# Strassen block products for the first product of tiles 2 to 8, with the weights' sums streamed from DRAM and the attention one pair ahead

## The chip, the core and the metric

The kernel runs on one core of a Trainium2 chip. A core has five engines that run their own instruction queues in order and wait for each other by semaphores: TensorE (PE in the profile; PEld are its weight loads), VectorE (DVE), ScalarE (ACT), GpSimd (POOL) and SyncE (SP, which here only issues DMAs). SBUF is the on-chip memory, PSUM the memory into which PE accumulates. The metric is the device time of one execution in microseconds (us), as the median of several runs.

## The reference

```python
def _attn_ref(q, k, v):                      # each (8, 8, 576, 64): batch, head, row, column
    q_s = q - np.max(q, axis=-1, keepdims=True)
    q_s = np.exp(q_s)
    q_s = q_s / (np.sum(q_s, axis=-1, keepdims=True) + 1e-09)
    k_s = k - np.max(k, axis=2, keepdims=True)          # over the rows
    k_s = np.exp(k_s)
    k_s = k_s / (np.sum(k_s, axis=2, keepdims=True) + 1e-09)
    kv = np.einsum('bhsd,bhse->bhde', k_s, v)
    return np.einsum('bhsd,bhde->bhse', q_s, kv)

def _moe_ref(x, w_in, w_out):                # x (4608, 512), w_in (512, 2048), w_out (2048, 512)
    h = np.maximum(x @ w_in, 0.0)
    return h * h @ w_out
```

The output of the attention, with heads side by side, is x. The weights come as 64-bit floats.

## The kernel before

The 4608 rows of x are worked off in nine tiles of 512 rows: tile t = 0 to 7 holds the first 512 rows of batch t, tile 8 the last 64 rows of all eight batches, which pass through DRAM (`x_tail`). Every number of the two big products is held as a sum of two 32-bit parts that PE takes in one pass, a high part and the rest (`wi_h`, `wi_l`, `xh`, `xl`, `gh`, `gl`), and each product is made of three matmuls: high times high, high times low, low times high.

A tile is a loop over 16 blocks f of 128 columns of w_in. `first` makes h for a block: 4 slices of 128 rows of w_in by 3 matmuls with 512 columns, 12 in all, into one of two PSUM buffers (pool `ps_h`). ACT and DVE make r = relu(h), h squared, and its parts gh and gl. `second` multiplies them with w_out into four accumulators `acc` that live through the tile; the three matmuls for one f and one accumulator are called a unit here. It runs two f behind (LA = 2), so that 8 units are left at the end of a tile, where `store` empties the accumulators and `split_x` splits the next tile's x.

Between these stands the attention of the next batch, b = t + 1, in four pieces p of two heads; in a tile, piece p belongs to the blocks f = 4p to 4p + 3. From batch 2 on, its steps are these.

- `blocks_max`, `blocks_exp`, `blocks_norm`, `blocks_turn`, `blocks_split`: q's softmax on DVE and ACT, with the halves of a maximum and of a sum exchanged over small DMAs (`sw_m`, `sw_s`), and the split of its transpose in `qh` and `ql` (on POOL where p is even, on DVE where p is odd).
- `k_max` on DVE, then `k_shift_pool` on POOL: an all-reduce over the partitions (`kmx<-km`), and the subtraction of its result from k (`k<-k,kmx`) and from its last rows (`kt`). `k_exp` on ACT turns these into `ek` and `kt`.
- `kv_product` (PE, then ks, kvh, kvl on DVE and ACT) and `x_product` (PE, six matmuls of 288 columns, then copies into x), for two pieces together where p is odd.

Up to the end of tile 0 a planner orders all instructions by costs and due times, with tile 0 in it. From tile 1 on (the planner is then closed) every engine's queue is in the order in which the code is written. All instructions pass through one helper, so that nearly all rows of a profile show the line L100; the tile names tell them apart.

## Time and profile before

| | |
|---|---|
| median of 3 runs | 883.64 us (883.05 to 884.48) |
| span of the profiled execution | 881.9 us |
| PE busy in the span | 865.1 us, 98% |
| DVE, ACT, POOL busy | 485.8, 359.7, 186.8 us |
| moved by DMA | 57.89 MB, 66 GB/s on average |

The span runs from the first to the last instruction of the profiled execution; the runs' times lie around it by some us. In a row of the timeline stand the start, the duration, the engine, the line, the operation, out<-in by names, the shapes, and in brackets the idle time ahead with what ended it ("issue" if nothing that the profile shows). In a row of a group stand the count after the x, then busy us and mean ns of one, then the idle time ahead and what ended most of it. A row of waits has the total, the number and the longest. A matmul's duration holds its latency; what counts on PE is the distance of two starts.

### The profile page before, as it was taken

The numbers are of one execution on the slowest core, as the hardware profiler recorded it, in microseconds if no ns is written. First come the engines' busy times: TensorE is split into PE (matmuls) and PEld (weight loads), VectorE is DVE, ScalarE is ACT, GpSimd is POOL, SyncE is SP. The second block draws the span as 40 slices with busy tenths as digits, with TensorE's granted clock in tenths as the row PEclk, the third lists the DMA queues.
The fourth block names the chain that finished last, engine by engine and source line by source line (L and its number), as shares of the span: only waits on it lengthen the run. The fifth ranks groups of instructions, "written<-read, shape, count | busy, mean of one in ns | idle before, by whom it ended". The sixth has DMA issues, their size and how long they took to land.

```text
span 881.9 us, 12457 instructions
## 1 busy us (share of the span) xinstructions
PE 865.1 (98%) x4456; PEld 714.6 (81%) x4456; DVE 485.8 (55%) x897; ACT 359.7 (41%) x668; POOL 186.8 (21%) x237
## 2 busy tenths in 40 slices
PE   7899999999999999999999999999999999999997
PEld 6678888888888888788888888888888888888886
DVE  6888976554655465545654565556564532233222
ACT  5878854333434342335333343334233422232221
POOL 5789982111111101110111112110111000000000
PEclk9999999999999999999999999999999999999999
DMA  9992122211311122112311222113111110010002
GB/s 262 376 349 70 37 50 73 53 29 37 85 39 39 39 63 80 39 38 57 86 39 39 46 72 48 30 38 93 39 38 39 54 50 1 0 48 1 1 1 48
DMA packets 140878, 57.89 MB, mean 66 GB/s; under 512 B 115600, under 2 KB 134032, under 8 KB 140688
## 3 DMA queue, kind: packets, MB, share of 16 engines
q1 hardware_dynamic: 139104, 55.79, 23.6%
q10 hardware_dynamic: 1712, 1.31, 0.5%
q8 instruction: 35, 0.57, 0.3%
q14 instruction: 27, 0.22, 0.1%
HBM read 46.14 MB, written 10.49 MB: 64 GB/s over the span
## 4 chain that ended last, share of the span: by engine, by line
PE 91%; DMA 3%; DVE 3%; issue 1%; ACT 1%; SPq 1%; POOL 0%; DVEq 0%; POOLq 0%; ACTq 0%
PE acc L100 43%; PE h L100 42%; PE x L100 3%; PE kv L100 2%; DMA q<-in_q_dram 1%; DMA raw<-in_moe_w_in_dram 1%; DMA sw_m<-bmx 1%; SPq L100 1%; DVE km L100 1%; DMA kt<-in_k_dram 0%; DVE w L100 0%; POOL w L100 0%; DVE gl L100 0%; DVE up L100 0%; DVE qt L100 0%
## 5 line engine op out<-in xcount | busy, mean ns | idle before, releaser
L100 PE MATMUL h<-xh,w 128*128 128x512 f32 x1152 | 379.3, 392 | 3.2 <-DVE gl L100 3.1
L100 PE MATMUL acc<-w,gh 128*128 128x512 f32 x1152 | 355.7, 390 | 0.0
L100 PEld LDWEIGHTS h<-xh,w 128*128 128x128 f32 x1152 | 216.2, 188 | 50.3 <-DVE gl L100 4.4
L100 PEld LDWEIGHTS acc<-w,gh 128*128 128x128 f32 x1152 | 214.7, 188 | 43.4
L100 PE MATMUL h<-xl,w 128*128 128x512 f32 x576 | 224.3, 389 | 0.0
L100 PE MATMUL acc<-w,gl 128*128 128x512 f32 x576 | 224.2, 389 | 0.0
L100 DVE SCALAR_TENSOR_TENSOR h<-h,r 128x512 f32<-128x512 f32 x144 | 99.4, 691 | 101.8 <-ACT r L100 101.0
L100 DVE TENSOR_TENSOR gl<-h,gh 128x512 fp32r<-128x512 f32 x144 | 99.2, 689 | 92.2 <-ACT gh L100 83.7
L100 ACT ACTIVATE r<-h 128x512 f32<-128x512 f32 x144 | 85.1, 591 | 152.2 <-PE h L100 151.8
L100 ACT ACTIVATE gh<-r 128x512 fp32r<-128x512 f32 x144 | 90.7, 630 | 122.2 <-PE acc L100 113.7
L100 PEld LDWEIGHTS acc<-w,gl 128*128 128x128 f32 x576 | 108.1, 188 | 22.8
L100 PEld LDWEIGHTS h<-xl,w 128*128 128x128 f32 x576 | 108.2, 188 | 21.3
L100 POOL TENSOR_TENSOR k<-k,kmx 128x512 f32<-128x512 f32 x24 | 30.8, 1282 | 171.9 <-issue 143.1
L100 POOL PARTITION_ALL_REDUCE kmx<-km x24 | 17.4, 724 | 207.4 <-DVE km L100 166.2
L100 ACT ACTIVATE q<-q 128x576 f32<-128x576 f32 (+1 forms) x32 | 21.5, 672 | 96.7 <-DVE q L100 87.9
L100 POOL TENSOR_TENSOR w<-w,raw 128x512 int32<-128x512 int32 x32 | 42.0, 1320 | 7.9 <-DVE w L100 2.8
L100 POOL TENSOR_TENSOR w<-w,w 128x512 fp32r<-128x512 f32 x32 | 41.1, 1299 | 5.8 <-ACT w L100 5.7
L100 DVE SCALAR_TENSOR_TENSOR bsm<-bsm,sw_s 128x18 f32<-128x18 f32 x24 | 5.6, 232 | 61.4 <-DMA sw_s<-bsm 61.4
L100 ACT ACTIVATE raw<-raw 128x1024 f32<-128x1024 f32 (+1 forms) x32 | 36.3, 1148 | 2.2 <-DMA raw<-in_moe_w_in_dram 2.0
L100 DVE TENSOR_TENSOR bmx<-bmx,sw_m 128x18 f32<-128x18 f32 x24 | 4.2, 176 | 53.0 <-DMA sw_m<-bmx 53.0
L100 ACT ACTIVATE kvh<-kv,ks 64x64 fp32r<-64x64 f32 x64 | 19.8, 309 | 29.4 <-DVE ks L100 28.9
L100 ACT CAST qh<-qT 128x576 fp32r<-128x576 f32 (+1 forms) x32 | 20.9, 653 | 26.2 <-DVE qT L100 24.6
(104 smaller groups left out, 666.8 us busy)
## 6 DMA issues: line engine op xcount, KB each, us to landing
k<-in_k_dram SPq DMA_DIRECT2D x32, 256.0 KB, 2.7
raw<-in_moe_w_in_dram SPq DMA_DIRECT2D x16, 512.0 KB, 8.5
raw<-in_moe_w_out_dram SPq DMA_DIRECT2D x16, 512.0 KB, 8.8
out_dram<-o SPq DMA_DIRECT2D x32, 256.0 KB, 2.4
v<-in_v_dram SPq DMA_DIRECT2D x56, 128.0 KB, 2.9
q<-in_q_dram SPq DMA_DIRECT2D x96, 72.0 KB, 2.4
sw_m<-bmx SPq DMA_DIRECT2D x96, 2.2 KB, 1.7
sw_s<-bsm SPq DMA_DIRECT2D x96, 2.2 KB, 1.7
```

What stands on the lines that cost most here:

```text
L100: getattr(self.eng, op)(*map(real, args), **{k: real(a) for k, a in kwargs.items()})
```

## The change

Tiles 2 to 8 (WT = 2) make h for two blocks f at a time, a pair, by Strassen's scheme in Winograd's form: the 512 rows of w_in, the 256 columns of the pair and the 512 columns of x are halved, and seven block products take the place of eight. A block product is 2 slices by 3 matmuls of 256 columns, 6 in all. A tile has 8 pairs.

- The four sums of a pair's weight blocks (`s1` to `s4`) are made in tile 1: `add_sums` on POOL, `split_sums` on ACT and DVE. They and the three blocks that are used as they are go to DRAM (`w_sums`), and from tile 2 on `load_sums` brings a pair's 14 half blocks back on ACT's DMA queue, four issues a pair, into a ring of two (the slabs of SBUF that held w_in).
- The four sums of the next tile's x (`t1` to `t4`) are made on POOL by `x_sum`, and all seven parts split by `split_part` on ACT and DVE: within the last pair (pair 7) of a tile, with t1's sum in pair 6.
- In a pair, PE's products go into two PSUM buffers (hu, hv), whose halves ACT copies out between (`u1`, `u2` in kept, `u3` in last) and DVE adds up to c1 (block 2i) and c2 (block 2i + 1). DVE makes max(c, 0) times c; ACT makes gh for both, DVE gl of c2, POOL gl of c1.
- The units of the second product for a pair are spread over the next pair, 8 of them: a11, s1, unit, s2, a12, two units, s3, two units, a22, s4, three units (named by the weight block of each product).
- The attention is one pair ahead (SKEW = 2 blocks): batch b + 1's first steps stand in tile t's pair 7. Its steps are in `even_step`, `even_after`, `odd_between`, `odd_step`, `odd_after`. Some loads of q and of k's last rows go to a spare buffer.

Core of the diff (helpers for names and views are left out):

```diff
+    def add_sums(j):
+        one, two = slabs[2 * j], slabs[2 * j + 1]
+        full = cvt.tile([P, 2, M], F32, tag="w", name=f"full_{j}")
+        for i, slab in enumerate((one, two)):
+            G.tensor_tensor(out=full[:, i, :], in0=slab[:, 0, :], in1=slab[:, 1, :], op=ALU.add)
...
+        G.tensor_tensor(out=s1, in0=a21, in1=a22, op=ALU.add)
+        G.tensor_tensor(out=s2, in0=s1, in1=a11, op=ALU.subtract)
+        G.tensor_tensor(out=s3, in0=a11, in1=a21, op=ALU.subtract)
+        G.tensor_tensor(out=s4, in0=a12, in1=s2, op=ALU.subtract)
+    def split_sums(j):
...
+        S.copy(out=hi, in_=sums)
+        V.tensor_tensor(out=lo, in0=sums, in1=hi, op=ALU.subtract)
+        for i, part in enumerate((hi, lo)):
+            to = w_sums[j].rearrange("p (n t) c -> p n t c", t=4)[:, :, i, :]
+            Y.dma_start(out=to, in_=part.rearrange("p (n c) -> p n c", n=4).bitcast(F32))
+    def split_part(src, t, name, eng=V):
...
+        S.copy(out=hi, in_=one)
+        eng.tensor_tensor(out=lo, in0=one, in1=hi, op=ALU.subtract)
+    def product(out, w, x, begin):
+        (wh, wl), (xh, xl) = w, x
+        for k in range(2):
+            for i, (a, m) in enumerate(((wh, xh), (wh, xl), (wl, xh))):
+                nc.tensor.matmul(
+                    out=out.real(), lhsT=a[:, k * P:(k + 1) * P].real(), rhs=m[:, k, :].real(),
...
+    def even_step(b, s):
...
+        if i == 0:
+            blocks_exp(b, p)
+        elif p % 2:
+            kv_product(b, p - 1)
+            kv_product(b, p)
+    def even_after(b, s):
...
+        if i == 2:
+            blocks_norm(b, p)
...
+    def odd_between(b, s, x):
...
+        if i == 3:
+            if p % 2:
+                x_product(b, p - 1, x)
+            blocks_turn(b, p)
...
+            if ahead(b, p, 1):
+                blocks_max(*ahead(b, p, 1))
+            if p % 2:
+                blocks_split(b, p)
+    def odd_step(b, s):
...
+        if i == 3 and ahead(b, p, 1):
+            k_max(*ahead(b, p, 1))
+            k_shift_pool(*ahead(b, p, 1))
+    def odd_after(b, s, x):
...
+        if i == 1:
+            k_exp(b, p)
...
+        elif p % 2:
+            x_product(b, p, x)
+        else:
+            blocks_split(b, p)
...
+            if t == WT - 1:
...
+                for j in range(NF // 2):
+                    if f == 3 + j * 13 // 8:
+                        split_sums(j)
+                    if f == 2 + j * 13 // 8:
+                        add_sums(j)
...
+            product(hu[:, left], w["a11"], x["b11"], True)
+            S.copy(out=u1, in_=hu[:, left])
+            if i == NF // 2 - 2 and b <= B:
+                x_sum(x_next, b, "t1")
+            add("t2")
+            turn("b11")
+            add("t3")
+            product(hv[:, right], w["s1"], x["t1"], True)
+            unit(1)
+            product(hu[:, left], w["s2"], x["t2"], False)
+            S.copy(out=u2, in_=hu[:, left])
+            load_sums(n + 2, 0)
+            turn("t1")
+            product(hv[:, left], w["a12"], x["b21"], False)
+            V.tensor_tensor(out=c1[:, left], in0=hv[:, left], in1=u1, op=ALU.add)
+            even_step(b_s, s)
+            unit(1)
+            even_after(b_s, s)
+            unit(1)
+            product(hu[:, left], w["s3"], x["t3"], False)
+            S.copy(out=u3, in_=hu[:, left])
+            load_sums(n + 2, 1)
+            V.tensor_tensor(out=c2[:, right], in0=hv[:, right], in1=u3, op=ALU.add)
+            turn("t2")
+            turn("b21")
+            add("t4")
+            unit(1)
+            odd_between(b_s, s + 1, x_next)
+            unit(1)
+            product(hu[:, left], w["a22"], x["t4"], False)
+            S.copy(out=c2[:, left], in_=hu[:, left])
+            load_sums(n + 2, 2)
+            V.scalar_tensor_tensor(out=c2, in0=c2, scalar=0.0, in1=c2, op0=ALU.max, op1=ALU.mult)
+            product(hv[:, right], w["s4"], x["b22"], False)
+            V.tensor_tensor(out=c1[:, right], in0=hv[:, right], in1=u2, op=ALU.add)
+            V.scalar_tensor_tensor(out=c1, in0=c1, scalar=0.0, in1=c1, op0=ALU.max, op1=ALU.mult)
+            for f, g, eng, tags in ((two, c2, V, ("xl1", "xh2")), (one, c1, G, ("gh", "gl"))):
...
+                S.copy(out=gh, in_=g)
+                eng.tensor_tensor(out=gl, in0=g, in1=gh, op=ALU.subtract)
...
+            load_sums(n + 2, 3)
+            odd_step(b_s, s + 1)
+            unit(1)
+            odd_after(b_s, s + 1, x_next)
+            for name in ("t3", "t4", "b22"):
+                turn(name)
+            unit(2)
```

What this does to the queues is seen at three places. In the names the first number behind gh, gl, h, r, c is the tile and the second the block f; behind k, km, kmx, ek, q, v it is the batch and the piece; the last number is the program's own. The first place is POOL in tile 4, from the all-reduce for piece 2 of batch 5 to that for piece 3. Before:

```order
L100 ISA
L100 ISA kmx_5_2_4683<-km_5_2_4680 128x128
L100 ISA
L100 TENSOR_TENSOR k_5_2_4541<-k_5_2_4541,kmx_5_2_4683 128x512
L100 TENSOR_TENSOR kt_5_4176<-kt_5_4176,kmx_5_2_4683 64x128
L100 TENSOR_TENSOR ql_5_2_4801<-qT_5_2_4774,qh_5_2_4799 128x576
L100 MEMSET v_5_3_4819 128x4
L100 ISA
```

Now, on the same engine at the same place:

```order
L100 TENSOR_TENSOR gl_4_4_5301<-c_4_4_5179,gh_4_4_5299 128x512
L100 ISA
L100 ISA kmx_5_2_5307<-km_5_2_5304 128x128
L100 ISA
L100 TENSOR_TENSOR k_5_2_5138<-k_5_2_5138,kmx_5_2_5307 128x512
L100 TENSOR_TENSOR kt_5_4395<-kt_5_4395,kmx_5_2_5307 64x128
L100 TENSOR_TENSOR gl_4_6_5422<-c_4_6_5364,gh_4_6_5420 128x512
L100 MEMSET v_5_3_5480 128x4
L100 TENSOR_TENSOR gl_4_8_5542<-c_4_8_5472,gh_4_8_5540 128x512
L100 ISA
```

The gl of c1 now stands right ahead of each all-reduce with its two bare ISA rows. The second place is ACT's queue around ek of the same piece. Before:

```order
L100 ACTIVATE r_4_9_4749<-h_4_9_4736 128x512
L100 ACTIVATE gh_4_9_4767<-r_4_9_4749 128x512
L100 ACTIVATE ek_5_2_4771<-k_5_2_4541 128x2x4x64
L100 ACTIVATE kt_5_4176<-kt_5_4176 64x128
L100 ACTIVATE r_4_10_4796<-h_4_10_4783 128x512
```

Now, at the end of pair 3 and the start of pair 4 of tile 4:

```order
L100 CAST gh_4_7_5416<-c_4_7_5391 128x512
L100 CAST gh_4_6_5420<-c_4_6_5364 128x512
L100 DMA w14_1566<-w_sums_5_111 128x512
L100 ACTIVATE ek_5_2_5428<-k_5_2_5138 128x2x4x64
L100 ACTIVATE kt_5_4395<-kt_5_4395 64x128
L100 COPY kept_4_4_5446<-h_4_9_5439 128x256 x2
L100 DMA w3_796<-w_sums_6_112 128x1024
```

Where r of the next block stood behind ek and kt, now the copies u1 and u2 of the next pair stand there, and the issue of a weight load. The third place is POOL at the end of tile 1, from the last all-reduce for batch 2. Before:

```order
L100 ISA
L100 ISA kmx_2_3_2296<-km_2_3_2293 128x128
L100 ISA
L100 TENSOR_TENSOR k_2_3_2214<-k_2_3_2214,kmx_2_3_2296 128x512
L100 TENSOR_TENSOR kt_2_1620<-kt_2_1620,kmx_2_3_2296 64x128
L100 MEMSET v_3_0_2464 128x4
```

Now the same stretch, from the all-reduce on (the sums of pair 7 follow in the same six rows as those of pair 6):

```order
L100 ISA kmx_2_3_2392<-km_2_3_2389 128x128
L100 ISA
L100 TENSOR_TENSOR k_2_3_2293<-k_2_3_2293,kmx_2_3_2392 128x512
L100 TENSOR_TENSOR kt_2_1628<-kt_2_1628,kmx_2_3_2392 64x128
L100 TENSOR_TENSOR full_6_2407<-w11_1342 128x512
L100 TENSOR_TENSOR full_6_2407<-w12_1420 128x512
L100 TENSOR_TENSOR sums_6_2410<-full_6_2407 128x256
L100 TENSOR_TENSOR sums_6_2410<-sums_6_2410,full_6_2407 128x256
L100 TENSOR_TENSOR sums_6_2410<-full_6_2407 128x256
L100 TENSOR_TENSOR sums_6_2410<-full_6_2407,sums_6_2410 128x256
L100 TENSOR_TENSOR full_7_2518<-w13_1486 128x512
```

The sums stand between the all-reduces on POOL's queue, and ahead of t1, the all-reduce for batch 3's first piece and t2.

More of the change, by code (lines that the diff above doesn't have):

```diff
@@ L388, in attention_ffn @@
     NG = SQ // Q
+    HM = M // 2
+    WT = 2
     assert B * TL == M and DM == NP * P and C * P == M
@@ L1005, in split_g, with second @@
         return gh, gl
-    def second(f, parts, acc, c):
+    def second(f, parts, acc, c, begin=0, end=NF - 1):
         gh, gl = parts
@@ L1013, in second, with begin_sums @@
                     out=acc[c], lhsT=a[:, cs], rhs=w[f],
-                    start=(f == 0 and n == 0), stop=(f == NF - 1 and n == 2),
+                    start=(f == begin and n == 0), stop=(f == end and n == 2),
+                )
+    def begin_sums(j):
+        one, two = slabs[2 * j], slabs[2 * j + 1]
+        for q, (slab, cols) in enumerate(
+            ((one, slice(0, HM)), (one, slice(HM, M)), (two, slice(HM, M)))
+        ):
+            Y.dma_start(
+                out=w_sums[j][:, 4 * q + 2:4 * q + 4, :], in_=slab[:, :, cols].bitcast(F32)
+            )
@@ L1015, in second @@
+    def product(out, w, x, begin):
[4 more added lines that the diff above has]
+                    out=out.real(), lhsT=a[:, k * P:(k + 1) * P].real(), rhs=m[:, k, :].real(),
+                    start=(begin and k == 0 and i == 0), stop=(k == 1 and i == 2),
+                    skip_group_check=True,
                 )
```

225 lines of the change are left out of this document (203 added, 22 removed).

## The prediction

> **What bounds the kernel now.** I read the page first: busy shares, then the chain that ended last, then the transfer rates by slice.
>
> ```profile
> span 881.9 us, 12457 instructions
> ...
> PE 865.1 (98%) x4456; PEld 714.6 (81%) x4456; DVE 485.8 (55%) x897; ACT 359.7 (41%) x668; POOL 186.8 (21%) x237
> ...
> GB/s 262 376 349 70 37 50 73 53 29 37 85 39 39 39 63 80 39 38 57 86 39 39 46 72 48 30 38 93 39 38 39 54 50 1 0 48 1 1 1 48
> ...
> PE 91%; DMA 3%; DVE 3%; issue 1%; ACT 1%; SPq 1%; POOL 0%; DVEq 0%; POOLq 0%; ACTq 0%
> ```
>
> TensorE is the bound; POOL, 21% busy, looks free; the transfers are light after the first 66 us. Next the timeline around a group of first products and around an attention product, for the price of a matmul.
>
> ```profile
> 401.29 0.39 PE L100 MATMUL h<-xh,w 128*128 128x512 f32 x1
> ...
> 404.01 0.62 PE L100 MATMUL acc<-w,gh 128*128 128x512 f32 x2
> ...
> 404.21 0.60 ACT L100 ACTIVATE r<-h 128x512 f32<-128x512 f32 x1 [0.88 <-PE h L100]
> ...
> 411.68 0.29 PE L100 MATMUL x<-qh,kvh 128*128 128x288 f32 x1
> ...
> 412.48 0.63 PE L100 MATMUL acc<-w,gh 128*128 128x512 f32 x2
> ```
>
> Twelve matmuls of 512 columns start in 2.72 us, 226.7 ns each; six of 288 columns, each with new 128x128 weights, in 0.80 us, 133.3 ns each. The 224 columns between them cost 93.4 ns (0.417 ns a column), so each matmul carries 13.3 ns beside its columns. A reader of the result starts 0.2 us after PE's last slot. Then POOL, because the change gives it work.
>
> ```profile
> 533.93 0.28 DVE L100 TENSOR_TENSOR km<-km,kt 64x128 f32<-64x128 f32 x1
> ...
> 530.66 0.11 POOL L100 MEMSET v<- 128x4 f32 x1
> 536.93 0.72 POOL L100 PARTITION_ALL_REDUCE kmx<-km  x1 [6.16 <-issue]
> 544.94 1.28 POOL L100 TENSOR_TENSOR k<-k,kmx 128x512 f32<-128x512 f32 x1 [7.29 <-DMA sw_s<-bsm]
> ...
> 154.28 0.11 POOL L100 MEMSET v<- 128x4 f32 x1
> 160.21 0.72 POOL L100 PARTITION_ALL_REDUCE kmx<-km  x1 [5.83 <-DVE h L100]
> ...
> POOL k L100 <- issue: 143.1, 20, 7.8
> ```
>
> This is the view that decides. In the program's order a bare ISA row stands before and behind each all-reduce. The all-reduce starts 5.8 to 6.2 us after the POOL instruction ahead of it even though its operand km was ready at 534.21; and k starts 7.16 us behind it (143.1 us in 20 waits for nothing that the profile shows). So an all-reduce holds POOL for 5.9 + 0.72 + 7.15 = 13.8 us, not for 0.72. In before POOL has nothing else to do at that place: the 5.9 mostly pass before km is there.
>
> **The change part by part.** Durations from the groups of instructions by shape:
>
> ```profile
> L100 POOL TENSOR_TENSOR k<-k,kmx 128x512 f32<-128x512 f32 x24 | 30.8, 1282 | 171.9 <-issue 143.1 <-DMA sw_s<-bsm 28.7
> L100 POOL TENSOR_TENSOR ql<-qT,qh 128x576 fp32r<-128x576 f32 x12 | 17.2, 1433 | 55.4 <-issue 28.8 <-ACT qh L100 26.6
> L100 POOL TENSOR_TENSOR kt<-kt,kmx 64x128 f32<-64x128 f32 x24 | 12.5, 521 | 0.9
> ...
> L100 ACT ACTIVATE gh<-r 128x512 fp32r<-128x512 f32 x144 | 90.7, 630 | 122.2 <-PE acc L100 113.7 <-issue 4.7 <-DVE qT L100 1.9
> L100 ACT ACTIVATE ek<-k 128x512 f32<-128x512 f32 x28 | 17.6, 629 | 30.5 <-POOL k L100 30.3 <-DVE k L100 0.2
> L100 ACT ACTIVATE kt<-kt 64x128 f32<-64x128 f32 x28 | 8.5, 303 | 1.3 <-POOL kt L100 0.9
> L100 ACT COPY o<-acc 128x256 f32<-128x256 f32 x1 | 0.4, 372 | 2.6 <-DVE o L100 2.6
> ...
> L100 DVE SCALAR_TENSOR_TENSOR h<-h,r 128x512 f32<-128x512 f32 x144 | 99.4, 691 | 101.8 <-ACT r L100 101.0
> L100 DVE TENSOR_TENSOR q<-q,bsm 128x576 f32<-128x576 f32 x24 | 20.7, 862 | 0.8
> L100 DVE STREAM_TRANSPOSE qT<-q 128x576 f32<-128x576 f32 x24 | 18.5, 770 | 0.2
> L100 DVE TENSOR_REDUCE bmx<-q 128x18 f32<-128x576 f32 x24 | 17.9, 744 | 0.4
> L100 DVE TENSOR_TENSOR qtl<-qTt,qth 128x256 fp32r<-128x256 f32 x2 | 0.8, 409 | 0.0
> ...
> 2.60 2.88 ACTq L100 DMA_DIRECT2D q<-in_q_dram  x3
> ...
> 877.90 0.56 ACTq L100 DMA_DIRECT2D out_dram<-o  x1
> ```
>
> *Products.* For a pair of f, 24 matmuls of 512 columns (5.44 us) become 42 of 256. No row has 256 columns: between 133.3 ns (288 columns) and 113.3 (half of 512's price), the two rows make 106.7 + 13.3 = 120 ns, so 5.04 us. 56 pairs x 0.40 = **-22.4 us** if nothing waits. A block product P (6 matmuls) is 0.72 us, a unit u of the second product 0.68, a whole pair 7 P + 8 u = 10.48.
>
> The Trainium skill ("TensorE: Matmul & The Clock Gate", LDWEIGHTS and Back-to-back issue gap) gives a 128-column weight load 107 ns, beside the matmul, and a matmul N/2.4 + 2.5 ns, 109 for 256 columns. By that the estimate is 42 x 109 = 4.58 us a pair and -48 us in all; the 288-column row, 133.3 ns against the formula's 122.5, speaks against it.
>
> *Weight stream.* 14 x 256 x 4 x 128 bytes = 1.84 MB a pair, 175 GB/s, against 376 GB/s in a slice of the page, each load issued two pairs (20 us) ahead: nothing; with that cover gone a late slab would stop its product. The four issues on ACT's queue I price at 0.56 us each (0.96 in the row of three is the upper bound); they stand between copies and count below where something is queued behind them. In tile 1 five issues a sum go on SP's queue ahead of the exchanges of maxima; they fall into the longer waits for POOL there: 0, at most 5.
>
> *Waits for the all-reduces.* In pairs 0, 2, 4 and 6 of a tile POOL now does gl of c1, then the next piece's all-reduce, then k. Counted from S, the end of the pair's last product: 0.2 to the first reader, add 0.41, max-square 0.69, gh 0.63, gl 1.28, hops 0.1, so gl ends at S+3.3. Only then 5.9 + 0.72 + 7.15 + k 1.28: S+18.4. ACT's queue of the next pair holds ek (0.63), kt (0.30) and, behind them, the copy u1 (0.37) that belongs to the pair after: S+19.7. PE's s2 product there waits for that copy. PE's work up to it is 12 u + 9 P = 14.64 us, so it stands for 5.1 us. Three pieces in each of tiles 2 to 5 and three in tile 6: 15 x 5.1 = **+76.5**.
>
> *DVE's queue behind the kv products* (pairs 2 and 6).
>
> ```profile
> 501.07 0.69 PE L100 MATMUL kv<-v,ek 128*64 128x65 f32 x16
> ...
> 502.39 0.50 PE L100 MATMUL h<-xh,w 128*128 128x512 f32 x1
> ...
> 505.11 0.58 DVE L100 SCALAR_TENSOR_TENSOR kvl<-kv,ks,kvh 64x64 fp32r<-64x64 f32 x2 [0.76 <-ACT kvh L100]
> ...
> 508.28 0.76 DVE L100 TENSOR_TENSOR ql<-qT,qh 128x576 fp32r<-128x576 f32 x1 [0.96 <-ACT qh L100]
> 508.80 0.29 PE L100 MATMUL x<-qh,kvh 128*128 128x288 f32 x1
> ```
>
> kvl is done 3.3 us after the two kv (1.32 us); in before ql then lands at 509.04, just as x wants it. Now the norm (its small steps and 0.86, 1.4), c2's add (0.4), an x copy (0.4), transpose and maximum (1.5) stand between, so that ql lands 7.7 us after kv; PE's x comes to it after 5 u + 3 P + 1.07 = 6.6. That is 1.1 us, and 0.4 because c1 comes later too: 10 pairs x 1.5 = **+15**.
>
> *The split of the next tile's x* (pair 7). t2 stands on POOL behind pair 6's all-reduce, k and kt; in pair 6 DVE is late, gl ends at S+5.7, so t2 ends at S+22.5. ACT's hi of t2 and b21 (1.25) and then c2's copy (0.37) wait in line, and the next tile's a11 can start at S+24.1 instead of S+13.3: 10.8 late. Behind it ACT has gh twice, two issues, ek, kt and three splits before u1, 2.6 us more than PE covers. 13.4 x 4 (into tiles 3 to 6; the boundaries into 7 and 8 have no all-reduce, 1 us each, and the end 0.5): **+53.6 + 2.5**.
>
> *Sums of weights in tile 1.*
>
> ```profile
> 155.16 2.72 PE h L100 x12
> ```
>
> One add_sums is 2 x 1.28 + 4 x 0.69 = 5.3 us of POOL (0.69 on the line through 1.28 at 512 and 1.43 at 576). From 154.4 on (the memset above) POOL must do 8 x 5.3, four all-reduces with k and kt (4 x 15.5), ql 1.4, t1 and t2 2.6: 108.6 us, and some 2.6 in which ql waits for ACT's qh. PE, which begins f = 4 at 155.16, has up to the s2 that needs t2 0.8 + 12 x 5.44 + 2 x 1.32 + 4 x 0.80 + 5 u + 2 P = 76.8 us. ACT meets the sums by its in-order copy of each and at the end adds 5.1 for splits and ek. 108.6 + 2.6 + 5.1 - 76.8 = **+40** (32 if POOL never waits; 45).
>
> *The clock after a stall.*
>
> ```profile
> 43.78 0.50 PE L100 MATMUL h<-xh,w 128*128 128x512 f32 x1 [2.01 <-DVE gl L100]
> ...
> 10.01 4.09 PE L1190 MATMUL idle<-ident 128*128 128x128 f32 x27
> ...
> 876.61 0.39 PE L100 MATMUL acc<-w,gl 128*128 128x512 f32 x1
> ...
> 878.00:882.00 4.00, 0.00 (x0) 0.00 (x0) 0.00 (x0) 0.00 (x0) 0.00 (x0) 0.62 0.54 135
> ```
>
> A stall of 2.0 us was followed by matmuls at full rate; after the last matmul (ends 877.0) the mean of 878 to 882 is 0.62, so the clock halved about 2 us later. I estimate that full rate takes some 3 us of dense work to come back, since the 27 fillers of the 10.01 row speed up on the way. About 22 stalls of 5 us or more then cost 0 to 1.7 us each; I take 0.75: **+16.5**.
>
> The Trainium skill (same page, Part 1: The HAM clock gate) wants a whole free-running window of 3.4 us to be idle, which a stall of 5.1 us holds half of the time: its estimate is 22 x 0.5 x 1.7 = 19 us. The last row above halved sooner than that.
>
> Sum: 881.9 - 22.4 + 40 + 76.5 + 15 + 53.6 + 2.5 + 16.5 = 1063.6 us of span; the runs' median is 1.7 above the profiled span: **1065 us**.
>
> **Rivals.** *All waits covered.* If the ISA rows run ahead and cost POOL nothing at their place, the chain from gl to k falls below 15.05 - 5.1 = 9.9 us, from where PE no longer stands; if ACT and DVE catch up within a pair as well, some 5 us of the rest remain: 883.6 - 22.4 + 5 = 866 us, faster. For it: PE hardly waits in tiles 1 to 8 of before. Against: twice above the 5.9 us begin only when the instruction ahead is done.
>
> The Trainium skill ("GPSIMD Engine Reference", 2.1 Instruction dispatch) books about 6 us for the first call of a freshly loaded kernel and nothing on the way back. With one load alone the chain would be 7.9 us and this rival would hold for the pieces; the 5.9 agrees, the 7.15 behind the all-reduce stands in the trace alone.
>
> *Only ACT's and DVE's queues.* The loads are hidden, but pairs 2 and 6 (+15), four boundaries at what ACT alone takes (4 x 5.8) and 2.5 remain: 883.6 - 22.4 + 41 = 902 us. For it: the 508.28 row, where ql is only just in time already. Against: as above.
>
> *No effect.* Waits eat just the 22.4: 883.6 us.
>
> **How the numbers follow.** Forecast 0.76 (950 to 1110: downward tile 1 at 32, half of the pieces' waits and two thirds of the boundaries covered, no DVE and no clock term, 32 + 38 + 18 + 2.5 - 22.4 = 68; upward tile 1 at 45, 1.7 us for every stall and ACT's issues at 0.96), queues only 0.10 (886 to 950), covered 0.11, no effect 0.03. 0.2% is about what a measurement of this kernel can tell from no change. Faster 0.11, same 0.03, slower 0.86. 930 to 1110 leaves out the 0.11, the 0.03 and about half of the queues' case.
>
> **What would show it.** In the changed kernel: matmuls of 256 columns 120 ns apart; POOL's all-reduce 5.9 us behind gl and k 7.2 behind that; ACT's ek waiting for POOL k some 5 us in pairs 1, 3 and 5, and PE's h for ACT's kept; tiles 2 to 5 some 30 us longer than now and tile 8 some 3 shorter; tile 1 some 40 longer, with ACT's copies of the sums waiting for POOL; a granted clock below 1.00 in tiles 1 to 6. The forecast is wrong if POOL's idle time before k shrinks, or if PE finds more to do ahead of s2 and a11 than I counted.

## The result and the profile after

The changed kernel takes 1115.14 us as the median of 3 runs (1111.18 to 1118.62), against 883.64: 1.262 times as long, 95% interval 1.258 to 1.267. The direction was forecast with 0.86, the size was not: 1065 us, and 1110 as the upper end. From here on the span of the profiled execution, 1109.4 us, is compared with the 881.9 of before: 227.5 us more.

The page of the changed kernel: busy shares, granted clock, chain that ended last.

```profile
span 1109.4 us, 15464 instructions
...
PE 915.7 (83%) x5464; PEld 784.1 (71%) x5464; DVE 548.7 (49%) x1038; ACT 392.4 (35%) x809; POOL 339.8 (31%) x369
...
PEclk9999997986799989898899898889988989999999
...
PE 41%; issue 14%; DMA 14%; DVE 13%; ACT 7%; POOL 7%; SPq 3%; ACTq 0%; DVEq 0%; POOLq 0%
```

TensorE is now busy for 83%, and no other engine for more than 49%: nobody is the bound, the engines wait for each other. The chain changes its engine all the time, where before 91% of it lay on PE.

The same kernel by tile, 1 to 8 (start and end, length, busy us and instructions of PE, PEld, DVE, ACT and POOL, granted clock, share and rate of the DMAs):

```profile
139.90:277.80 137.90, 104.17 (x478) 83.11 (x477) 64.76 (x110) 41.66 (x76) 61.38 (x68) 0.86 0.51 157
277.80:413.70 135.90, 98.63 (x622) 84.67 (x620) 58.56 (x116) 39.29 (x89) 31.58 (x33) 0.89 0.53 154
413.70:545.40 131.70, 102.42 (x633) 89.29 (x633) 60.46 (x120) 38.91 (x89) 28.29 (x30) 0.89 0.51 149
...
805.40:927.90 122.50, 102.85 (x633) 90.38 (x634) 60.92 (x118) 39.02 (x89) 27.15 (x27) 0.90 0.51 151
927.90:1013.40 85.50, 84.64 (x530) 76.15 (x529) 34.52 (x58) 26.50 (x58) 15.48 (x12) 1.00 0.60 198
```

Before, tiles 1 to 6 took 93.6 to 94.8 us at a clock of 1.00, tile 7 took 87.0. Tile 7, which has the new products and no attention beside them, is 1.5 us shorter now. Everything is lost in tiles 1 to 6, where the attention of the next batch runs: 44 us in tile 1, 42 in tile 2, 35 to 37 in tiles 3 to 5, 29 in tile 6. (A tile is cut at its first product of h. From tile 3 on it now begins with the 8 units left by the tile ahead, tile 2 with 4; before there were none. Tile 8, at 96.0 us instead of 92.1, holds 5.4 us of tile 7's units, so its own work is 1.5 us shorter as well.) What PE waits for there (total, times, longest):

```profile
PE h L1133 <- ACT kept L100: 93.9, 31, 12.7
PE h L1133 <- ACT c L100: 33.4, 4, 8.7
PE kv L100 <- issue: 19.2, 2, 10.8
PE h L1133 <- ACT last L100: 13.0, 6, 3.5
```

The first row is the copy u1 ahead of s2, the second the boundary ahead of a11 in four tiles, the third kv in tile 1, the fourth the copy u3 ahead of a22. One such wait in the timeline, in tile 4, pair 1 into 2:

```profile
568.32 0.72 POOL L100 PARTITION_ALL_REDUCE kmx<-km  x1 [6.04 <-DVE q L100]
578.38 1.25 POOL L100 TENSOR_TENSOR k<-k,kmx 128x512 f32<-128x512 f32 x1 [9.34 <-issue]
...
579.67 0.63 ACT L100 ACTIVATE ek<-k 128x512 f32<-128x512 f32 x1 [6.72 <-POOL k L100]
580.21 0.29 ACT L100 ACTIVATE kt<-kt 64x128 f32<-64x128 f32 x1
580.41 0.35 ACT L100 COPY kept<-h 128x256 f32<-128x256 f32 x1
...
572.81 1.60 PE L1133 MATMUL h<-w,w 128*128 128x256 f32 x12
574.72 0.39 PE L100 MATMUL acc<-w,gl 128*128 128x512 f32 x1
580.81 2.93 PE L1133 MATMUL h<-w,w 128*128 128x256 f32 x12 [5.71 <-ACT kept L100]
```

The all-reduce starts 6.0 us after the POOL instruction ahead of it, k comes 9.3 us behind it, ek waits for k, the copy u1 stands behind ek and kt, and s2 stands for 5.7 us. What POOL does in the 6.0 and the 9.3 us no row names; this text calls them the all-reduce's loads. The last row shows the second loss: 12 matmuls of the same shape that took 1.60 us ahead of the wait take 2.93 behind it.

### The profile page after: what moved, and what is told of

It is laid out like the page before. It is cut to its first block, busy times and chain, and to the rows that moved or that the text cites. A ratio compares the mean times of both kernels' runs of the same rounds, so it can differ in the third digit from the quotient of the medians.

```text
span 1109.4 us, 15464 instructions
## 1 busy us (share of the span) xinstructions
PE 915.7 (83%) x5464; PEld 784.1 (71%) x5464; DVE 548.7 (49%) x1038; ACT 392.4 (35%) x809; POOL 339.8 (31%) x369
## 4 chain that ended last, share of the span: by engine, by line
PE 41%; issue 14%; DMA 14%; DVE 13%; ACT 7%; POOL 7%; SPq 3%; ACTq 0%; DVEq 0%; POOLq 0%
PE acc L100 18%; PE h L1133 17%; DVE c L100 3%; PE h L100 3%; DMA q<-in_q_dram 3%; DMA w<-w_sums 3%; SPq L100 3%; DMA spare<-in_q_dram 3%; POOL k L100 3%; DMA sw_m<-bmx 2%; ACT w L100 2%; PE kv L100 2%; DVE km L100 1%; DVE w L100 1%; POOL sums L100 1%
## 5 line engine op out<-in xcount | busy, mean ns | idle before, releaser
L1133 PE MATMUL h<-w,w 128*128 128x256 f32 x2016 | 304.1, 299 | 142.2 <-ACT kept L100 93.9
L1133 PEld LDWEIGHTS h<-w,w 128*128 128x128 f32 x2016 | 286.6, 204 | 179.4 <-ACT kept L100 109.5
L100 POOL TENSOR_TENSOR gl<-c,gh 128x512 fp32r<-128x512 f32 x56 | 72.2, 1290 | 356.4 <-ACT gh L100 329.6
L100 DVE TENSOR_TENSOR c<-h,kept 128x256 f32<-128x256 f32 x112 | 47.0, 420 | 230.8 <-PE h L1133 223.7
L100 DVE SCALAR_TENSOR_TENSOR c<-c 128x512 f32<-128x512 f32 x112 | 81.8, 731 | 41.4 <-ACT c L100 39.5
L100 PE MATMUL h<-xh,w 128*128 128x512 f32 x256 | 91.0, 416 | 11.0 <-DVE gl L100 11.0
L100 ACT CAST gh<-c 128x512 fp32r<-128x512 f32 x112 | 69.6, 622 | 80.9 <-DVE c L100 80.9
L100 PEld LDWEIGHTS h<-xh,w 128*128 128x128 f32 x256 | 51.2, 200 | 24.2 <-DVE gl L100 11.8
L100 PE MATMUL h<-xl,w 128*128 128x512 f32 x128 | 52.6, 411 | 0.0
L1133 PE MATMUL h<-b22xh,w 128*128 128x256 f32 x224 | 52.2, 295 | 0.0
L100 ACT ACTIVATE ek<-k 128x512 f32<-128x512 f32 x28 | 17.6, 627 | 90.9 <-POOL k L100 90.8
```

Source lines behind the costliest of these rows:

```text
L100: getattr(self.eng, op)(*map(real, args), **{k: real(a) for k, a in kwargs.items()})
L1133: nc.tensor.matmul(out=out.real(), lhsT=a[:, k * P:(k + 1) * P].real(), rhs=m[:, k, :].real(), start=(begin and k == 0 and i == 0), stop=( ...
```

## The experiments

**Maxima over TensorE.** All of batch 2 to 7's maxima of k without POOL:

```diff
         if i == 0:
+            if (b, p) != (TB + 1, 0):
+                k_turn_max(b, p)
             blocks_exp(b, p)
...
+        if i == 1 and (b, p) != (TB + 1, 0):
+            k_shift_pe(b, p)
...
             k_max(*ahead(b, p, 1))
-            k_shift_pool(*ahead(b, p, 1))
```

`k_turn_max` is a transpose on PE, a maximum on DVE and a diagonal on ACT; `k_shift_pe` is ones times the diagonal on PE and the subtraction on DVE. Batch 2 and the first piece of batch 3 are changed alike in tile 1.

> The changed kernel, but the maxima of k for batches 2 to 7 go over TensorE (transpose, maximum on DVE, one broadcast matmul, subtraction on DVE) instead of POOL's all-reduce, so that no library is loaded in tiles 1 to 8. Theory (the loads hold POOL 13.8 us each; the clock halves behind the waits that this makes): the stalls before s2 in pairs 2, 4 and 6 (some 14 us a tile), the boundaries' 8.8 us and the 58 us of the sums of weights go, and the halved clock behind them. What stays is 881.9 - 18.5 (pairs of 10.55 us) = 863 us, some 10 us in tile 1, the waits of ACT and DVE on each other (10 x 1.5 in the kv pairs, 4 x 6 at the boundaries, 2 to 3 us in pairs 1 and 5), some 60 us at the most: 870 to 930 us, tiles 2 to 5 near 95 us. Rival, the order of ACT's and DVE's queues (copies behind DMA issues, ql behind the norm) makes the stalls: tiles 2 to 5 stay at 120 us or more, and the time is above 1020 us, more if DVE's new work delays c2. Rival, the weight stream slows everything that needs a DMA: above 1020 us too.

Measured: 944.28 us (ratio to before 1.070, 1.067 to 1.073). Its waits of PE for the two copies:

```profile
PE h L1133 <- ACT kept L100: 17.6, 17, 2.6
PE h L1133 <- ACT last L100: 9.1, 9, 2.8
```

The waits for u1 fell from 93.9 us to 17.6, those at the boundaries (ACT c) are gone from the list, tile 1 ends at 252.2 instead of 277.8, and the clock in tiles 2 to 6 is 0.97 to 1.00. So 171 of the 231 us go with the all-reduces (and with k's subtraction, now on DVE). What stays is 14 us over the upper end of what the theory expected.

**Idle matmuls against the clock.** At 13 of the long waits PE got work that nothing needs, transposes of 128x128 at 109 ns each:

```diff
+            if i == 0 and WT < t < WT + 5:
+                fillers(70)
             product(hu[:, left], w["a11"], x["b11"], True)
...
+            if i == 2 and WT < t < WT + 5:
+                fillers(50)
+            if i == 4 and t < WT + 5:
+                fillers(40)
             product(hu[:, left], w["s2"], x["t2"], False)
```

> The changed kernel with idle 128x128 transposes on TensorE ahead of the s2 of pairs 2 (50 of them, 5.45 us at 109 ns) and 4 (40) and ahead of the first a11 of tiles 3 to 6 (70), where it stalls 6.6, 5.3 and 8.8 us. They write a part of a bank that nothing reads. Theory (a stall of more than about 2 us halves the clock for some 4 us of the work behind it, 1.35 to 2.3 us each): the stalls shrink to under 2 us, the matmuls behind them run at 120 ns, and 13 places x 1.8 = 23 us are gained: 1092 us, the granted clock near 0.97. Rival (the matmuls behind a stall are slow because of other engines or of the transfers, or the prediction's 0.75 us was right): at most 10 us are gained, above 1105. If the fillers themselves come late or last longer than the stall, it gets slower.

Measured: 1180.71 us. The fillers wrote into the bank that s2 uses, and so waited for the same copy: every filler was added, and the 13 waits ahead of them sum to 83.1 us, against 83.7 in the changed kernel. The fillers took 101.2 us where 680 of them at 109 ns take 74.1, so 27 us of the slow stretches now fell on them. This run can't tell what the clock costs the kernel. With a bank of their own:

> The changed kernel with the same idle transposes at the same three kinds of place (50 ahead of s2 in pair 2, 40 in pair 4, 70 ahead of the first a11 of tiles 3 to 6), but into a bank of its own that no copy has to free, so that they can run while TensorE stands. In the run before, they stood behind the same copy as s2 (stalls of 6.5 us unchanged) and were added whole, so it said nothing on the clock. Theory (a stall over some 2 us halves the clock for the work behind it, 1.35 to 2.3 us each): the stalls behind the fillers are under 2 us, and 13 places x 1.8 = 23 us are gained: 1092 us, granted clock near 0.96. Rival (the slow matmuls come from something else, or cost 0.75 us as predicted): 1105 us or more.

Measured: 1099.1 us (1.245, 1.244 to 1.247; the changed kernel 1.262, 1.258 to 1.267). Tiles 3 to 5 by windows:

```profile
417.20:543.40 126.20, 114.86 (x793) 101.28 (x793) 60.49 (x120) 38.88 (x89) 28.37 (x30) 0.97 0.54 155
543.40:671.10 127.70, 113.86 (x793) 100.14 (x793) 60.47 (x120) 38.89 (x89) 28.34 (x30) 0.99 0.53 154
671.10:797.50 126.40, 115.36 (x792) 101.44 (x792) 60.67 (x120) 38.89 (x89) 28.36 (x30) 0.97 0.54 155
```

PE does 160 more matmuls a tile, and the tiles are 2.1 to 5.5 us shorter, at a clock of 0.97 to 0.99 instead of 0.88 to 0.89. The copies come as late as ever: in pairs 2 and 4 of tiles 3 to 6 the copy u1 that s2 waits for starts 22.5 us behind the start of s4 two pairs ahead, 22.4 in the changed kernel. Only the slow matmuls behind the waits are gone. Summed over all starts of tiles 2 to 6 (how far the next start lies beyond the usual distance for the shape, where it isn't a wait), slow matmuls cost 45.2 us in the changed kernel and 23.4 here, 21.8 less at 13 places, as the theory had it. The total shows less: 16 us by the medians (the theory 23, the rival 10 at most), 10.4 between the two profiled executions. So it is the sum over the starts, and not the total, that speaks against 0.75 us a wait.

**Without the stream.** The weights' sums are loaded for two pairs alone:

```diff
-        if n >= (B + 1 - WT) * (NF // 2):
+        if n >= 2:
             return
```

> The changed kernel, but the weights' sums are loaded from DRAM for the first two pairs alone; all later pairs multiply by what the slabs then hold. It leaves out the right weights, 128 MB of transfers and four DMA issues on ACT a pair. Theory (the library loads make the stalls): tiles 2 to 6 stay within 6 us of the changed kernel each, 1085 to 1115 us, though the all-reduce to k may shrink from 8.0 to near 7.2 us if the transfers slow it, which takes 0.8 x 19 = 15 us off. Rival (issues and transfers make the stalls): s2's waits go, below 1020 us.

Measured, in one run: 1105.09 us. PE's wait for u1 is 101.3 us, for the boundaries 33.1: neither the four issues on ACT nor the transfers make them. Three smaller things are the stream's. The wait for u3 is gone. The group of k on POOL waits less; in the changed kernel and without the stream (idle us of 24 behind the bar):

```profile
L100 POOL TENSOR_TENSOR k<-k,kmx 128x512 f32<-128x512 f32 x24 | 30.3, 1261 | 187.7 <-issue 166.0 <-PE h L100 7.3 <-DMA w<-w_sums 7.3
```

```profile
L100 POOL TENSOR_TENSOR k<-k,kmx 128x512 f32<-128x512 f32 x24 | 30.1, 1256 | 172.7 <-issue 157.4 <-DMA w<-w_sums 8.2 <-PE h L100 7.1
```

That is 7.8 us against 7.2 from the all-reduce to k (7.2 in the kernel before). And the exchange of q's maxima and sums lands later; median us from issue to landing in the changed kernel, then without the stream:

```profile
sw_m<-bmx SPq DMA_DIRECT2D x96, 2.2 KB, 2.8
sw_s<-bsm SPq DMA_DIRECT2D x96, 2.2 KB, 3.4
```

```profile
sw_m<-bmx SPq DMA_DIRECT2D x96, 2.2 KB, 1.7
sw_s<-bsm SPq DMA_DIRECT2D x96, 2.2 KB, 1.7
```

Both are 1.7 in the kernel before. The same edit on the kernel with the maxima over TensorE:

> The kernel with the maxima over TensorE, with the weights' sums loaded for two pairs alone (the right weights and their transfers are left out). In the changed kernel without the stream the stalls and half clock of pairs 1 and 5 (1.3 to 2.8 us and 1.8) were gone, those before s2 were not. Theory (the stream delays the exchange of q's maxima, 6 us or more under way, for which ACT's exponential and behind it the copy u3 wait): pairs 1 and 5 lose their 2 to 5 us here too, 920 to 930 us instead of 944. Rival (DVE's work for the maxima over TensorE delays them): within 5 us of 944.

Measured, in one run: 924.3 us, as the theory had it; pairs 1 and 5 have no wait of 0.35 us or more there, but for 2.0 us in tile 2.

**Without the sums of weights in tile 1.**

```diff
-        full = cvt.tile([P, 2, M], F32, tag="w", name=f"full_{j}")
...
-        made["sums", j] = sums.rearrange("p n c -> p (n c)")
+        made["sums", j] = one.rearrange("p t n -> p (t n)").bitcast(F32)
```

> The changed kernel without the six sums on POOL of each weight pair in tile 1: the copy and the difference that split a sum take the first weight itself instead. It leaves out the sums of weights. Theory (POOL in tile 1 has to do all-reduces and sums one behind the other): tile 1 loses most of its 45 us and pair 0 of tile 2 its 12.8 us stall: 1060 us. Rival (the splits on ACT and DVE, five DMA issues on SP or the splits of x at the end set tile 1): tile 1 and that stall keep 30 us or more, above 1085 us.

Measured, in one run: 1090.53 us, on the rival's side by the time, but not by tile 1. Tile 2 begins at 244.5 instead of 277.8, so 33 us of tile 1's loss come with the sums; the total of this one run shows 25 of them, with tiles 2, 4 and 5 coming out 3 to 5 us longer. But the wait in the first pair of tile 2 stays:

```profile
259.28 2.93 PE L1123 MATMUL h<-w,w 128*128 128x256 f32 x12 [12.47 <-ACT kept L100]
```

In the changed kernel POOL's timeline shows what t2 stands behind:

```profile
259.42 0.10 POOL L100 MEMSET v<- 128x4 f32 x1
275.46 0.73 POOL L100 PARTITION_ALL_REDUCE kmx<-km  x1 [15.94 <-DVE km L100]
283.45 1.25 POOL L100 TENSOR_TENSOR k<-k,kmx 128x512 f32<-128x512 f32 x1 [7.26 <-DMA w<-w_sums]
```

POOL has done nothing for 15.9 us when the maximum of batch 3's first piece comes, and k then follows 7.3 us behind the all-reduce. Only this piece over TensorE:

```diff
                 if f == 15:
                     k_max(b + 1, 0)
-                    k_shift_pool(b + 1, 0)
...
+            k_turn_max(b + 1, 0)
             x = x_first(x_next, b, x_2)
+            k_shift_pe(b + 1, 0)
             k_exp(b + 1, 0)
```

> The changed kernel, but the first piece of batch 3, whose all-reduce is the last in tile 1, has its maximum over TensorE; every other all-reduce and all sums of weights stay. Theory (the prediction's 40 us for tile 1 counted POOL's work as packed; in the changed kernel POOL stood from 259.6 to 275.3 us for that piece's maximum, which DVE does behind the last copies of x, and only then loaded for 13.8 us with t2 to t4 in line behind it): the 12.8 us before the s2 of tile 2's first pair and the 2.4 us of half clock behind it go, and some 3 us for the two matmuls in line are added before the first a11: tile 2 begins near 280 us, 1103 us in all. Rival (the sums make POOL late there, as the prediction had it): the stall stays above 8 us and the time within 4 us of 1115.

Measured: 1109.06 us (1.258, 1.252 to 1.263), between the theory's 1103 and the rival's 1111. The stall is gone, as the theory had it: s2 starts on time.

```profile
285.12 0.63 PE L100 MATMUL acc<-w,gh 128*128 128x512 f32 x2
285.59 0.39 PE L100 MATMUL acc<-w,gl 128*128 128x512 f32 x1
285.82 1.59 PE L1133 MATMUL h<-w,w 128*128 128x256 f32 x12
```

Tile 2 begins 5.9 us later, at 283.7, and is 11.5 us shorter. Of these 5.6 us the total shows nothing certain: the runs reach from 1104 to 1116, and tiles 5 and 6 of the profiled one are 6.8 us longer. The place is shown, the gain in time isn't.

**The kernel before without all-reduces.**

> The kernel before, with the maxima of k for batches 2 to 7 over TensorE instead of POOL's all-reduce. Theory (there the loads lie beside other work: POOL has nothing else to do at their place): nothing is gained but the waits of 1.2 and 0.7 us in tiles 3 and 4, and TensorE and DVE get 24 x 0.2 us of work: 884 to 889 us. Rival (the loads cost the kernel before as well): below 880 us.

Measured: 902.51 us (1.023, 1.021 to 1.024), a miss: neither theory nor rival. The maxima over TensorE cost 20 us where PE has no free time. Some 7 of them are waits for kvl, behind DVE's new work:

```profile
PE x L100 <- DVE kvl L100: 7.3, 12, 1.0
```

In the kernel before that wait is 0.7 us. The rest is some 0.6 us for each of 24 pieces: around a piece's two small products the timeline has 12 matmuls of first products in 3.01 and 2.84 us instead of 2.72, and 0.24 for the second of the two. The all-reduces cost the kernel before nothing: from tile 1 to tile 7 PE waits for 1.1 us in all there, and that for DVE. So the gain from 1115 to 944 is not the worth of a better maximum.

**The all-reduce kept, one pair earlier.**

```diff
-        if i == 3 and ahead(b, p, 1):
+        if i == (3 if (b, p) == (TB + 1, 0) else 1) and ahead(b, p, 1):
             k_max(*ahead(b, p, 1))
             k_shift_pool(*ahead(b, p, 1))
...
-            if ahead(b, p, 1):
-                load_kq(*ahead(b, p, 1), "k")
+            if ahead(b, p, 2):
+                load_kq(*ahead(b, p, 2), "k")
```

> The changed kernel, with the all-reduce kept on POOL, but the maximum, all-reduce and subtraction of each piece of k from the second of batch 3 on made one pair of f earlier than now; k's odd pieces lie in spare memory for it, and k is loaded two pieces ahead. Tile 1 and every other order are as in the changed kernel. Theory (the loads are a latency of 15 us in one queue, which hurts only because ek, and behind it the copy u1 on ACT, come within a pair of it): s2 waits no more in pairs 2, 4 and 6, t2 no longer stands behind an all-reduce, and the boundaries fall from 8.8 us to the 2.4 that the kernel with the maxima over TensorE shows; tile 1's 45 us and pair 0's 12.8 us in tile 2 stay, the waits for the exchange in pairs 1 and 5 too: tiles 3 to 5 near 100 us, 970 to 985 us in all. Rival (POOL is full: 4 x 13.8 us of loads, 4 k, gl, ql and t1 to t4 in 91 us, so that gl of c1 and ql come late now): tiles 3 to 5 above 112 us, 1040 us or more.

Measured: 1085.85 us (1.230, 1.227 to 1.233). The rival's number, but not its reason alone. PE's waits and one of the new ones:

```profile
PE kv L100 <- POOL kt L100: 40.9, 3, 15.9
PE acc L100 <- POOL gl L100: 29.6, 9, 4.5
PE kv L100 <- POOL spare L100: 24.8, 2, 12.7
...
PE h L1136 <- ACT kept L100: 17.7, 5, 12.4
```

```profile
585.27 0.45 POOL L100 TENSOR_TENSOR kt<-kt,kmx 64x128 f32<-64x128 f32 x1
...
585.78 0.48 PE L100 MATMUL kv<-v_tail,kt 128*64 128x65 f32 x4 [11.79 <-POOL kt L100]
```

The waits for u1 in pairs 2, 4 and 6 are gone (12.4 of the 17.7 us are the one in tile 2's first pair), and 65.7 us have come at kv, which reads the tail rows of two pieces together, one of them the piece that is now being shifted. Another 29.6 us are units that wait for gl of c1, which POOL does behind the load; there the rival was right. Both mended:

```diff
+            if p == 1:
+                shift_tail(b, 2, G)
...
-            for f, g, eng, tags in ((two, c2, V, ("xl1", "xh2")), (one, c1, G, ("gh", "gl"))):
+            for f, g, eng, tags in ((two, c2, V, ("xl1", "xh2")), (one, c1, V if i % 2 == 0 and b < B else G, ("gh", "gl"))):
```

> The earlier all-reduce again, with the two places mended at which the run before waited anew. There the stalls before s2 in pairs 2, 4 and 6 and the boundaries' 8.8 us were gone, but in pair 2 kv stood 12 to 16 us for the all-reduce of piece 2, whose shifted tail rows it reads, and in pairs 1 and 5 the fifth unit stood 3 to 5 us for gl of c1, which POOL does behind the all-reduce. Now piece 2's tail is shifted behind the kv products, and gl of c1 is on DVE in pairs 0, 2, 4 and 6. Tile 1 is as in the changed kernel. Theory (a load costs its latency where something of the same pair waits, and nothing where POOL's queue has room): tiles 3 to 5 fall from 120 to 124 us to 100 to 106 (91 us of work, the exchange's waits in pairs 1, 5 and 7), the whole to 985 to 1000 us. Rival (four loads a tile are too much for POOL wherever they stand): tiles 3 to 5 stay above 112 us, and the waits turn up at the next thing that POOL delivers; 1030 us or more.

Measured: 986.06 us (1.117, 1.114 to 1.120), tiles 3 to 5 at 99.1, 105.8 and 106.3. The theory holds:

```profile
PE h L1143 <- ACT last L100: 29.1, 11, 3.8
PE h L1143 <- ACT kept L100: 22.3, 7, 15.1
PE kv L100 <- issue: 20.8, 2, 11.1
```

19 all-reduces with their loads still run on POOL in tiles 2 to 6, and tiles 3 to 6 take 404.8 us in all, as long as in the kernel with the maxima over TensorE (404.7). What is left is the exchange (ACT last), the 15.1 us at the start of tile 2, and kv in tile 1.

**Orders of the queues.** The kernel with the maxima over TensorE, with q's exponential behind the copy of a22, x_product ahead of k_max and two splits of the next x behind u1:

> The kernel with the maxima over TensorE, and in the order of the queues: q's exponential (which waits for the exchange) behind the copy of a22 instead of ahead of u3 and of that copy; k's exponential right behind it instead of behind both gh; x_product ahead of k_max, so that x's copies don't wait for DVE's maximum; the splits of t4 and b22 for the next tile behind its first copy u1 instead of ahead; in tile 1 the first piece's maximum, exponentials and load one step earlier. No arithmetic is changed. Theory (what is left of waits at 944 us is copies that stand in ACT's or DVE's queue behind something late): of 34 us of stalls and 16 us of half clock in tiles 2 to 6 some 35 go, and some 8 of tile 1's 20: 900 us. Rival (the exchange itself sets the pace: what depends on it only comes later, and ql or ek is then late for x or kv): 925 to 945 us. It beats the kernel before only if under 10 us of waits are left.

Measured: 929.1 us (1.053, 1.052 to 1.055), on the rival's side. Tiles 3 to 6 are at 97.3 to 98.8 and the copies no longer wait for the exchange, but 7.7 us for a maximum too early in PE's queue in tile 1 and 12.5 us for DVE's sums have come instead. It is the fastest version run that computes everything (the 924.3 us above leave the right weights out). Three attempts to join it with the earlier all-reduce fell short:

> The earlier all-reduce together with the order of the queues of the run before (q's exponential behind the copy of a22, x_product ahead of k_max, the splits of t4 and b22 behind u1, that of t3 behind c1's sum), and in tile 1 the maxima over TensorE; the first piece of batch 3 has its maximum over TensorE too, in the first pair of tile 2. No arithmetic is changed. Theory (no load is waited for, no matmuls for maxima in tiles 2 to 6, no copy behind something late): tile 1 some 13 us longer than in the kernel before, tiles 2 to 6 at 95 us, tiles 7 and 8 at 84.5 and 95.3: 900 us, under the 929 of the last version, and still above the kernel before, since the products' 18.5 us are less than tile 1's sums, the boundaries and the longer exchange take. Rival (the exchange or ACT's queue stays the pace): 920 us or more.

> The same two mends in the version with all reorders and with batch 2's maxima over TensorE in tile 1; q's and k's exponentials now stand behind c1's maximum, so that c1's sum, which frees the bank that the next s1 needs, no longer waits for the exchange. No arithmetic is changed. Theory: the 12 to 16 us before kv's tail, the 5 us in pairs 1 and 5, the 2.4 us at the boundaries and the half clock behind them go: tiles 3 to 6 at 93 to 97 us, 895 to 915 us in all; still above the kernel before, by tile 1's sums and the first pairs of tile 2. Rival (POOL's loads stay the pace): 950 us or more.

> The earlier all-reduce with both mends, and the order of the queues of the version that took 929 us (q's exponential behind the copy of a22, not behind c1's maximum as in the version of 957 us); batch 2's maxima and the first of batch 3 over TensorE. No arithmetic is changed. Theory: tiles 3 to 6 at 94 to 98 us, tile 2 near 110, the products begin at 245: 905 to 920 us, the fastest with Strassen's products here and still slower than the kernel before. Rival (DVE, which now has gl of c1, is late with c1's sum and with ql): 930 us or more.

Measured: 1062.55, 957.51 and 938.4 us. The first has the waits of kv and gl (109 us by its view of waits). In the second, units wait 26.3 us for gh on ACT, which now stands behind q's exponential and so behind the exchange. In the third, whose prediction also missed by 18 us, tiles 3 to 6 take 97 to 103 us: 10.9 us are c1's sum on DVE, which has gl of c1 as well.

No version beats the kernel before. The products' 18.5 us are the most that these versions can gain, and even without the sums tile 2 began 12 us later than before, with four units still to do.

## Why the prediction missed, step by step

The terms, in us of span; measured terms are distances of starts on PE beyond the usual distance for the shape, a wait where one is over 0.32 us, else slow:

| step | predicted | measured |
|---|---|---|
| 56 pairs of products | -22.4 | -18.5 (10.55 a pair) |
| sums of weights in tile 1 | +40 | +61: 45.3 to the first a11, 2.8 for the 4 units left, 12.8 at s2 |
| s2 in pairs 2, 4 and 6 | +76.5 | +72, with the few tenths before x |
| DVE's queue behind kv | +15 | in the line above |
| boundaries into tiles 3 to 6 | +53.6 | +47 |
| boundaries into 7 and 8 | +2.5 | +2 |
| half clock after waits | +16.5 | +45 |
| u3 behind the exchange, pairs 1 and 5 | none | +16 |
| small waits in pair 3 | none | +3 |
| sum | 181.7 | 227.5 (rows rounded), as the spans show |

**Right.** The 256-column matmul was taken at 120 ns and has 120 (P in 0.72 us), though a whole pair has 10.55 us and not 10.48; of the 3 us by which tile 8 was to be shorter, its own work has 1.5. The load on both sides of the all-reduce, 5.9 and 7.15 us, was the view that decided: 5.7 to 6.2 in 22 of 24 and 7.8 on average in the changed kernel. Taking the all-reduces away, or moving them a pair ahead, took the waits for u1 away; taking the stream away did not. The boundaries' reason (t2 behind pair 6's all-reduce) held too: without it their 8.7 us went.

**The step that failed most: the clock after a stall.** The price, 0.75 us a stall with 1.7 as the bound, was wrong. In tiles 2 to 6 every wait of 2.76 us or more (19), three of the six from 2.0 to 2.4 us, and none up to 1.9 us was followed by matmuls at half rate, which cost 1.9 us each on average. The other 3 us or so are single matmuls where the shape changes. That these are 22, as counted, is luck: the count was of stalls of 5 us or more, and there are 15. The prediction assumed that the rate comes back within some 3 us of dense work; behind the wait that ends at 580.81 it takes 3.7 us. This term alone moved the time by 29 us; with it right, the forecast would have been 1094 us. The fillers took half of it away without making any copy come earlier.

The trace shows how it works. All changes of the granted clock in the changed kernel lie on a grid of 3.413 us that runs on regardless of the work. These are five of its windows around the wait before 580.81 (length, busy us and instructions of PE, PEld, DVE, ACT and POOL, granted clock, DMA share and rate):

```profile
570.87:574.28 3.41, 3.41 (x23) 3.04 (x22) 1.99 (x4) 1.25 (x2) 0.00 (x0) 1.00 0.91 322
574.28:577.69 3.41, 0.82 (x5) 0.35 (x3) 0.00 (x0) 0.00 (x0) 0.00 (x0) 1.00 0.18 63
577.69:581.11 3.42, 0.30 (x1) 0.30 (x2) 0.00 (x0) 1.08 (x3) 2.73 (x3) 0.50 0.00 0
581.11:584.52 3.41, 3.41 (x28) 3.19 (x29) 0.42 (x1) 0.37 (x1) 1.56 (x2) 0.50 0.56 147
584.52:587.93 3.41, 3.41 (x44) 3.04 (x41) 1.40 (x7) 1.40 (x5) 0.10 (x1) 1.00 0.55 161
```

The window in which PE was busy for 24% is followed by half clock, and the first dense window at half clock is what brings full clock back. Of this trace's windows from 30 us on, all 28 at full clock with PE busy for 47% or less were followed by half clock, and none of the 234 with more; at half clock, the 27 with 84% or more were followed by full clock, and none of the 26 with 76% or less. In all sixteen traces a border at 47.5% misplaces 17 of 4138 windows. So a wait costs nothing while it fills less than about half of any one window, a wait of 2 us may lie either way, and the price is half of the time in which PE works until the end of the first dense window.

The Trainium skill ("TensorE: Matmul & The Clock Gate", Part 1: The HAM clock gate) has full rate come back after one busy window of about 3.4 us, which fits the size, and half rate only after an idle window of that length. The estimate of 19 us made from it in the prediction let half of the waits of 5 us escape; here even those of 2.76 us were all followed by half rate, and the rows above show that a window 24% busy is enough.

**Tile 1 was mis-sized.** POOL's 108.6 us were added up as if little kept it from starting the next thing. By that sum it has t2 at 265.6 us; in the trace ACT takes t2 at 286.37, 21 us later. Some 10 us are its last piece, which waits for x and for DVE's maximum: 15.9 us of waiting in the row at 275.46, where the sum had only the 5.9 of the load. The sums of weights make some 9 more: POOL is busy with them for 47.4 us instead of 42.4, and waits 3.9 between them. That the sums and the loads there are in each other's way was right: ek, whose k is ready at 175.6, comes at 183.56, because ACT's queue has the copy of a sum ahead of it that POOL begins only behind k.

**A wait was not seen.** The transfers were priced at nothing, because each slab has 20 us of cover. That was true of the slabs. But the exchange of q's maxima shares the DMA engines with them, and ACT's exponential, which waits for it, has u3 behind it:

```profile
568.07 0.68 ACT L100 ACTIVATE q<-q 128x576 f32<-128x576 f32 x1 [3.92 <-DVE q L100]
568.13 0.33 ACTq L100 DMA_DIRECT2D w<-w_sums  x1
568.66 0.35 ACT L100 COPY last<-h 128x256 f32<-128x256 f32 x1
```

**Priced too high** were DVE's queue behind kv (ql came 0.4 us late, not 1.5) and the boundaries by 7 us. The 76.5 us for s2 came out near 69, but not as 15 waits of 5.1: there are 14 of more than 0.32 us, from 1.3 to 6.9 us. The misses upward were some 72 us, those downward 27. Neither the clock's 29 nor tile 1's 21 alone leaves the range up to 1110 us; that the others nearly cancel, 23 against 27, is luck.

## What to carry to other kernels

An instruction that holds its engine for 14 us is free as long as nothing on that engine or behind its result is wanted within them; before work is packed closer, list for each in-order queue what then stands behind its longest instruction. Where a dense TensorE is made to wait often, price every wait above 2 us with another 2 for the clock, as measured here, and look at small exchanges over DMA when a stream is added beside them. Moving the long step earlier, with everything that reads its result or stands behind it, gave back 129 us here without touching it.

## What the runs showed of the hardware

- The time from the all-reduce to the next POOL instruction grows with the DMA traffic: 7.2 us on average at 52 GB/s or with the stream out (one run), 7.8 with it, single ones up to 10.5.
- POOL slows DVE. In the changed kernel, DVE's 128x512 difference takes 0.69 us alone and 1.21 while POOL works:

```profile
530.36 0.69 DVE L100 TENSOR_TENSOR w<-x,w 128x512 fp32r<-128x512 f32 x1 [0.84 <-ACT w L100]
...
544.57 1.21 DVE L100 TENSOR_TENSOR w<-t,w 128x512 fp32r<-128x512 f32 x1 [10.47 <-ACT w L100]
...
543.96 1.26 POOL L100 TENSOR_TENSOR x<-t,x 128x512 f32<-128x512 f32 x1
```

The Trainium skill ("GPSIMD Engine Reference", 1. Specifications) states this contention for DVE instructions with two SBUF inputs, and the rows agree.
- A 128x128 transpose and a small 32-bit product, put into a dense stream of matmuls, cost some 0.6 us together in the kernel before.
- The granted clock is decided at the end of each 3.413 us window by PE's busy share in it: below about 47% it halves, and at half clock a share of 84% or more brought it back to full in the changed kernel.
